# Batch index 1: the weight forms' first additions behind the remainder of g, and one cast moved to ACT

## The chip, the core and the metric

The kernel runs on one core of a Trainium2 chip. The metric is the device time of one execution in microseconds. The engines are TensorE (PE; its weight loads are listed apart as PEld), VectorE (DVE), ScalarE (ACT), GpSimd (POOL, unused but for setup) and SyncE (SP, which issues DMAs).

## The reference: an attention with 32 memories, then a gated product

For 8 batches of 8 heads, 576 rows and width 64, an attention first condenses keys and values with weights from `phi`, and then attends to the 32 condensed memories. Its output, as 4608 rows of 512, goes through two weight matrices with a silu between:

```
a = exp(phi - max(phi));  a = a / (sum(a) + 1e-9)
k_m, v_m = a^T k, a^T v                       # 32 memories per head
scores = q k_m^T / 8
attn = exp(scores - max(scores));  attn = attn / (sum(attn) + 1e-9)
x = attn v_m                                  # 4608 x 512
h = x @ w_in                                  # 512 x 2048
g = h * (1 / (1 + exp(-h)))
out = g @ w_out                               # 2048 x 512
```

The product of attention with `v_m` and `w_in` is folded: the kernel multiplies the memories' values with `w_in` once per batch (a tile `pm`) and the attention's weights with that.

## The kernel before

Every factor of the large products is held as a high part (rounded to PE's fast 32-bit type) and a low part (the remainder), and a product is three: high x high, high x low, low x high. So each tile is first cast and then subtracted: the cast gives the high part, the subtraction the remainder.

A batch runs over 16 steps `fc` of 128 columns of the hidden width. In a step PE computes h (L698, twelve products); ACT takes silu of 512 rows into `gbuf` (L725) and of the 64 left-over rows into `gleft` (L727); `split` makes the two parts of g in `gparts` (L715 the cast on DVE, L717 the remainder on DVE; L713 would be the cast on ACT); one step later PE multiplies g with the matching rows of `w_out`, held as `wo_hi` and `wo_lo` (L743, twelve products: for each of four row tiles high x high, high x low, low x high, so the third product is the first that needs the remainder). h has one buffer: the next step's L698 can start when everything that reads h has read it.

Between these, the next batch's attention is worked off by a table of events, each with a batch and a step (a half is the step's second part). In batch 1 that is, for batch 2: the maximum and the exponent of phi (L258 to L319), the condensed keys and values (L335, L353 to L361, written beside h in h's own buffer), their transposition (L367 on PE, also beside h, then L368 and L369), the scores (L382, L389, L391), their maximum (L426), subtraction (L430), exponent (L434), sum (L438 to L440), division (L444), transposition (L464), and the split of the result (L472 on ACT, L479 on DVE). `p_mm` (L646) and its split (L674 on ACT, L676 on DVE) make `pm`.

Batches 2 to 7 use a form of the second product with fewer multiplications, which needs sums and differences of blocks of `w_out`. They are made in batch 1 by `w_forms`, for eight pairs of row tiles j = 0 to 7. Part 0, at the step 1.5 j + 2, is all on DVE: L811 restores 128 x 1024 weights from their two parts into `wf`, and L815 to L818 make four blocks of 128 x 256 from it. Part 1, at the step 1.5 j + 2.5, splits the result: ACT casts (L832) and DVE subtracts (L833), first one piece `t1` that is then stored in memory, then the pieces `kept`.

What sets the order: PE runs in the written order throughout. ACT does so from batch 1 on (`in_order(ACT)`), so an instruction of `w_forms` that waits on ACT holds up the next silu. In batch 0 DVE and ACT are held in order at its start, and later only by pairs. DVE in batch 1 is ordered by a scheduler when the program is built, within the dependencies; `behind(i, other)` adds a pure order between two instructions of one engine, with no wait. `last_split` is the list of all remainders of g written so far; its last entry is the newest.

Of the kernel before, what the change touches and what calls it, by code (L numbers as in the profile page):

```python
# [25 lines left out]
NFC = DFF // P  # L26
# [22 lines left out]
def attn_ffn_kernel(  # L49
# [37 lines left out]
    def load(dst, src, few=False, queue=None):  # L87
        i = (queue or nc.sync).dma_start(dst, src)
        if few:
            tc.add_manual_dep(  # L90
                i.ins,
                loads[-DEEP].ins.name,
                mybir.DependencyInfo(mybir.DependencyClass.Sync, mybir.DependencyReason.DATA),
                reason="few at a time",
            )
        loads.append(i)

    @contextmanager
    def in_order(*engines):
        traced = nc.cur_bb.bb.instructions  # L100
        n = len(traced)
        last = {}
        yield last
        for i in list(nc.cur_bb.bb.instructions)[n:]:
            if i.engine in engines:
                if i.engine in last:
                    tc.add_manual_dep(
                        i,
                        last[i.engine].name,
                        mybir.DependencyInfo(mybir.DependencyClass.NoSync, mybir.DependencyReason.DATA),  # L110
                        reason="in_order",
                    )
                last[i.engine] = i
# [6 lines left out]
    raws, cvas, last_silu, last_split, last_kvn, last_turn = {}, {}, [], [], [], []  # L120
# [562 lines left out]
    def ffn1(b, fc, h=None, low_last=False):  # L683

        hi, lo = pj[b, fc * P // JW]
        fs = slice(fc * P % JW, fc * P % JW + P)
        ahi, alo = at[b]["ahi"], at[b]["alo"]
        if h is None:
            h = live["h"] = ps.tile([P, 2, 512], F32, tag="h", name="h", bufs=1)
        kinds = ((hi, ahi), (hi, alo), (lo, ahi))  # L690
        todo = [(hf, k) for hf in range(2) for k in range(3)]
        if low_last:
            todo = [(hf, k) for k in (0, 2, 1) for hf in range(2)]
        n = [0, 0]
        for hf, k in todo:
            wt, a = kinds[k]
            for p in range(2):
                nc.tensor.matmul(  # L698
                    h[:, hf, :HALF], wt[:, p, fs], a[:, p, hf * HALF : (hf + 1) * HALF],
                    start=n[hf] == 0, stop=n[hf] == 5, skip_group_check=low_last,  # L700
                )
                n[hf] += 1
        return h
# [3 lines left out]
    def split(g32, steps=(0, 1), gs=None):  # L707
        if gs is None:
            n = next(turn) % 2
            gs = gparts[:, 0, n], gparts[:, 1, n]  # L710
        ghi, glo = gs
        if 2 in steps:
            nc.scalar.activation(ghi, g32, AF.Copy)  # L713
        if 0 in steps:
            nc.vector.tensor_copy(ghi, g32)  # L715
        if 1 in steps:
            last_split.append(nc.vector.tensor_tensor(glo, g32, ghi, op=ALU.subtract))  # L717
        return gs
# [3 lines left out]
    def silu(b, fc, h):  # L722
        g32 = gbuf.rearrange("p (n f) -> p n f", n=2)[:, next(half) % 2]
        w = MAIN // 2
        nc.scalar.activation(g32.rearrange("p (h f) -> p h f", h=2), h[:, :, :w], AF.Silu)  # L725
        o = b % 2 * LEFT
        i = nc.scalar.activation(  # L727
            gleft[:, fc, o : o + LEFT].rearrange("p (h f) -> p h f", h=2), h[:, :, w:HALF], AF.Silu
        )
        if b == 0 and fc > 1:  # L730
            last_silu.append(i)
        return g32
# [61 lines left out]
    def as_f32(x):  # L794
        return x.bitcast(F32)

    def keep(tag, n):
        t = sb.tile([P, n, DMODEL], F32R, tag=tag, name="kept", bufs=1)
        for i in range(n):
            kept.append(t[:, i])  # L800
            kept_at.append((t, i))

    def w_forms(j, step):


        if step == 0:
            while len(kept) < 3 * j + 3:
                keep(*homes_left.pop(0))
            f = at[0]["forms", j] = sb.tile([P, 2, DMODEL], F32, tag="cva", name="wf", bufs=1)
            c = slice(2 * j, 2 * j + 2)  # L810
            i = nc.vector.tensor_tensor(f, as_f32(wo_hi[:, c]), as_f32(wo_lo[:, c]), op=ALU.add)  # L811
            if j == 0:
                behind(i.ins, last_split[-1])
            b11, b12, b21, b22 = (f[:, k, q * Q : (q + 1) * Q] for k in range(2) for q in range(2))
            nc.vector.tensor_tensor(b11, b12, b11, op=ALU.subtract)  # L815
            nc.vector.tensor_tensor(b12, b22, b12, op=ALU.add)
            nc.vector.tensor_tensor(b22, b22, b11, op=ALU.add)
            nc.vector.tensor_tensor(b21, b22, b21, op=ALU.subtract)  # L818
            return
        f = at[0]["forms", j].rearrange("p k (q f) -> p (k q) f", q=2)  # L820
        t1 = sb.tile([P, 1, DMODEL], F32R, tag="cva1", name="t1", bufs=1)
        runs = [[t1, 0, 1]]
        for u in range(3 * j, 3 * j + 3):
            t, i = kept_at[u]
            if t is runs[-1][0]:
                runs[-1][2] = i + 1
            else:
                runs.append([t, i, i + 1])
        n = 0
        for t, i, e in runs:  # L830
            src, to = f[:, n : n + e - i], t[:, i:e]
            nc.scalar.activation(to[:, :, :Q], src, AF.Copy)  # L832
            nc.vector.tensor_tensor(to[:, :, Q:], src, to[:, :, :Q], op=ALU.subtract)  # L833
            n += e - i
        load(saved[j], as_f32(t1[:, 0]))
# [285 lines left out]
    with in_order(DVE, ACT) as last:  # L1121
# [71 lines left out]
        h = ffn1(0, 0, low_last=True)  # L1193
        g32 = silu(0, 0, h)
        w_conv(I1, None, "s")
        gs = split(g32, steps=(2,))
# [24 lines left out]
    def behind(i, other):  # L1221
        tc.add_manual_dep(
            i,
            other.ins.name,
            mybir.DependencyInfo(mybir.DependencyClass.NoSync, mybir.DependencyReason.DATA),
            reason="behind",
        )
# [30 lines left out]
    for b in range(B):  # L1258
        if b == 1:
            whole.close()  # L1260
            ctx.enter_context(in_order(ACT))
        for s in range(NFC if b > 1 else 0):
            t, j = divmod(s, NP)
            h = ffn1s(b, t, j)
            part = forms(b, t, j, h)
            run(b, s)
            finish(range(NI))
            prev = ("st", b, t, j, part)
        for fc in range(NFC if b < 2 else 0):
            if b == 0 and fc < 2:  # L1270
                for part in range(2):
                    for fn, a in events.pop((b, fc + part / 2), []):
                        fn(*a)
                continue
            h = ffn1(b, fc, low_last=b == 1 and fc == 0)
            gs = split(silu(b, fc, h))
            for part in range(2):
                if b == 0:
                    finish((2 * part, 2 * part + 1))
                traced = nc.cur_bb.bb.instructions  # L1280
                n = len(traced)
                late = set()
                for fn, a in events.pop((b, fc + part / 2), []):
                    m = len(nc.cur_bb.bb.instructions)
                    fn(*a)
                    if fn is phi_max:
                        late.update(i.name for i in list(nc.cur_bb.bb.instructions)[m:])
                if b == 0:
                    for i in list(nc.cur_bb.bb.instructions)[n:]:
                        if i.engine == ACT:  # L1290
                            behind(i, last_silu[-1])
                        elif i.engine == DVE and (fc > 10 or i.name in late):
                            behind(i, last_split[-1])
            if b:
                finish(range(NI))
            prev = ("main", b, fc, gs)
        if b % 2:
            for n in range(NLS):
                gs = left_split(b, n)
                if b > 1:  # L1300
                    run(b, NFC + n)
                finish((0, 1, 2, 3))
                prev = ("left", b, n, gs)
# [56 lines left out]
```

## Time and profile before

| | |
|---|---|
| median of three runs | 679.07 us (678.88 to 679.44) |
| the profiled execution | 679.03 us, of it 677.2 us from the first to the last instruction |
| PE busy | 667.9 us |
| DVE busy | 517.8 us |
| ACT busy | 369.1 us |
| mean granted PE clock | 0.999 |

In the profile a row of a list in order of time gives the start in us from the first instruction, the duration, engine, line, operation, the tile written and those read, the shape, and in brackets idle time ahead of it with what ended it. A row with x2 or x12 is that many alike in a row; the duration runs from the first's start to the last's end. Instructions of DVE and ACT can start a little before the one ahead has ended. Batch 1's steps take from about 106 to 189 us, and its left-over rows follow until about 202 us.

### The profile page before, as it was taken

What the parts mean: (1) busy time and instruction counts of PE and PEld (TensorE: products, weight loads), DVE (VectorE), ACT (ScalarE), POOL (GpSimd) and SP (SyncE); (2) the same over time, 40 slices, a digit from 0 to 9 for tenths busy, and PEclk for the clock granted to TensorE, in tenths of its full rate; (3) what the DMA queues carried; (4) which work ended last, traced back from release to release, by engine and by line L of the source; (5) the groups of instructions that cost most, each with busy time, mean ns of one, the idle gap of its engine ahead of it and who ended that gap; (6) DMA issues with size and microseconds to landing.
All of it is one profiled execution on the core that took longest, in us unless ns stands there. A gap on an engine that the chain in (4) does not pass through costs nothing.

```text
span 677.2 us, 14529 instructions
## 1 busy us (share of the span) xinstructions
PE 667.9 (99%) x5788; PEld 588.4 (87%) x5788; DVE 517.8 (76%) x1090; ACT 369.1 (54%) x682; POOL 0.7 (0%) x6
## 2 busy tenths in 40 slices
PE   8999999999999999999999999999999999999997
PEld 3578778787888998999988999899997999889996
DVE  4897899988938689868877688877877668867653
ACT  3878684533625556654655546564654646554441
POOL 0000000000000000000000000000000000000000
PEclk9999999999999999999999999999999999999999
DMA  9988985224270452243520534116430204300001
GB/s 338 373 321 293 313 307 184 82 109 145 85 231 18 185 180 102 79 180 124 178 95 16 184 102 177 66 48 231 157 126 32 86 2 156 114 27 17 32 1 47
DMA packets 37747, 93.92 MB, mean 139 GB/s; under 512 B 4656, under 2 KB 21168, under 8 KB 34096
## 3 DMA queue, kind: packets, MB, share of 16 engines
q1 hardware_dynamic: 36736, 90.22, 38.3%
q10 hardware_dynamic: 944, 2.77, 1.0%
q8 instruction: 46, 0.75, 0.5%
q14 instruction: 21, 0.17, 0.1%
HBM read 77.22 MB, written 15.73 MB: 137 GB/s over the span
## 4 chain that ended last, share of the span: by engine, by line
PE 78%; DVE 6%; ACT 1%; issue 1%; DVEq 0%; ACTq 0%
PE sum L890 34%; PE h L851 21%; PE acc L743 6%; PE lsum L972 5%; PE bg L646 3%; PE h L698 3%; PE accleft L743 2%; PE h L335 1%; PE bg L335 1%; PE bg L382 1%; PE pacc L646 1%; DVE gparts L717 1%; DVE pm L676 0%; DVE sc L430 0%; ACT aparts L879 0%
## 5 line engine op out<-in xcount | busy, mean ns | idle before, releaser
L851 PE MATMUL h<-aparts,pm 128*128 128x288 f32 x1152 | 168.7, 295 | 0.0
L851 PEld LDWEIGHTS h<-aparts,pm 128*128 128x128 f32 x1152 | 157.3, 188 | 0.7
L865 ACT ACTIVATE gbuf<-h 128x512 f32<-128x512 f32 x96 | 57.3, 597 | 117.2 <-PE h L851 113.9
L890 PE MATMUL sum<-wo_hi,aparts 128*128 128x256 f32 x384 | 102.5, 289 | 0.0
L890 PE MATMUL sum<-kept,aparts 128*128 128x256 f32 x576 | 100.1, 282 | 0.0
L890 PE MATMUL sum<-wo_lo,aparts 128*128 128x256 f32 x384 | 100.0, 282 | 0.0
L870 DVE TENSOR_TENSOR gbuf<-gbuf 128x256 f32<-128x256 f32 x96 | 40.6, 423 | 71.4 <-ACT gbuf L865 70.9
L879 ACT ACTIVATE aparts<-gbuf 128x512 fp32r<-128x512 f32 x86 | 54.4, 633 | 63.5 <-DVE gbuf L874 63.5
L743 PE MATMUL acc<-wo_hi,gparts 128*128 128x512 f32 x256 | 85.0, 397 | 0.2
L890 PEld LDWEIGHTS sum<-wo_hi,aparts 128*128 128x128 f32 x384 | 72.7, 189 | 11.5 <-ACT gleft L867 10.1
L890 PEld LDWEIGHTS sum<-kept,aparts 128*128 128x128 f32 x576 | 82.6, 191 | 0.0
L881 DVE TENSOR_TENSOR gparts<-gbuf,aparts 128x512 fp32r<-128x512 f32 x86 | 59.6, 693 | 19.6 <-ACT aparts L879 19.6
L890 PE MATMUL sum<-wo_hi,gparts 128*128 128x256 f32 x384 | 73.2, 281 | 0.0
L890 PEld LDWEIGHTS sum<-wo_lo,aparts 128*128 128x128 f32 x384 | 73.1, 190 | 0.0
L890 PE MATMUL sum<-kept,gparts 128*128 128x256 f32 x288 | 65.5, 282 | 0.0
L743 PEld LDWEIGHTS acc<-wo_hi,gparts 128*128 128x128 f32 x256 | 47.6, 188 | 14.2 <-DVE t L833 1.7
L890 PEld LDWEIGHTS sum<-wo_hi,gparts 128*128 128x128 f32 x384 | 59.4, 190 | 0.0
L698 PEld LDWEIGHTS h<-aparts,pm 128*128 128x128 f32 x372 | 51.8, 188 | 6.5 <-issue 2.7
L698 PE MATMUL h<-aparts,pm 128*128 128x288 f32 x372 | 56.1, 299 | 0.4 <-ACT aparts L611 0.4
L869 ACT ACTIVATE aparts<-gbuf 128x384 fp32r<-128x384 f32 x96 | 50.4, 525 | 0.0
L743 PE MATMUL acc<-wo_lo,gparts 128*128 128x512 f32 x128 | 49.4, 393 | 0.3 <-DVE wo_lo L182 0.2
L890 PEld LDWEIGHTS sum<-kept,gparts 128*128 128x128 f32 x288 | 47.9, 190 | 0.0
(212 smaller groups left out, 954.3 us busy)
## 6 DMA issues: line engine op xcount, KB each, us to landing
win<-win_saved SPq DMA_DIRECT2D x24, 1024.0 KB, 4.9
kv<-in_kv SPq DMA_DIRECT2D x28, 516.0 KB, 4.9
q<-in_q SPq DMA_DIRECT2D x16, 576.0 KB, 6.3
raw<-in_w_in SPq DMA_DIRECT2D x14, 512.0 KB, 7.5
raw<-in_w_out SPq DMA_DIRECT2D x6, 1024.0 KB, 6.6
win_saved<-win SPq DMA_DIRECT2D x4, 1024.0 KB, 8.7
phi<-in_phi SPq DMA_DIRECT2D x7, 576.0 KB, 8.5
out<-oo SPq DMA_DIRECT2D x26, 128.0 KB, 2.3
```

What stands on the lines that cost most here:

```text
L335: nc.tensor.matmul(pt[p][M * r : M * (r + 1), :KVW], e[:, p, c, M * r : M * (r + 1)], kvt[c][:, p, r], start=c == 0, stop=False, skip_grou ...
L646: nc.tensor.matmul((bg[p][M * r : M * (r + 1)] if beside else bg[M * r : M * (r + 1), p, :w]).rearrange("p (k f) -> p k f", f=P), kvT[D * ...
L698: nc.tensor.matmul(h[:, hf, :HALF], wt[:, p, fs], a[:, p, hf * HALF : (hf + 1) * HALF], start=n[hf] == 0, stop=n[hf] == 5, skip_group_chec ...
L743: nc.tensor.matmul(acc[key], gt[:, cs], wt[:, fc], start=fc == 0 and n == 0, stop=fc == NFC - 1 and n == 2)
L851: nc.tensor.matmul(h[:, i, :HALF], wt[:, p, f : f + P], a[:, p], start=n == 0, stop=n == 5)
L865: nc.scalar.activation(gbuf[:, :MAIN].rearrange("p (i f) -> p i f", i=2), h[:, :, :w], AF.Silu)
L869: nc.scalar.activation(hi[:, :3], g[:, 1:4], AF.Copy)
L870: nc.vector.tensor_tensor(g[:, 4:6], g[:, :1].broadcast_to([P, 2, P]), g[:, 1:3], op=ALU.subtract)
L879: nc.scalar.activation(hi[:, 3:], g[:, 4:], AF.Copy)
L881: last_split.append(nc.vector.tensor_tensor(lo[:, 3:], g[:, 4:], hi[:, 3:], op=ALU.subtract))
L890: nc.tensor.matmul(sums[bank][:, place * Q : (place + 1) * Q], gt[:, k], wt, start=bank not in begun, stop=True, skip_group_check=True,)
L972: nc.tensor.matmul(sums[k], part[gt][:, 2 * i + k], wt[:, fc], start=n == 0 and i == 0 and m == 0, stop=last and i == 1 and m == 2,)
```

## The change

Two edits. First, L811 of every j is put behind the newest remainder of g, where before only that of j = 0 was. Second, in the last step of the first batch, the cast of g is made by ACT (L713) and not by DVE; the remainder stays on DVE.

```diff
@@ w_forms, step 0
             i = nc.vector.tensor_tensor(f, as_f32(wo_hi[:, c]), as_f32(wo_lo[:, c]), op=ALU.add)
-            if j == 0:
-                behind(i.ins, last_split[-1])
+            behind(i.ins, last_split[-1])
@@ the loop over the steps of batches 0 and 1
             h = ffn1(b, fc, low_last=b == 1 and fc == 0)
-            gs = split(silu(b, fc, h))
+            gs = split(silu(b, fc, h), steps=(2, 1) if b == 0 and fc == NFC - 1 else (0, 1))
```

PE's and SP's orders stay as they were. After the change every line from L813 on has a number lower by one (L815 to L818 are L814 to L817, L833 is L832).

On ACT, at the end of the first batch, the order before was this (`gbuf` is silu of the 512 rows, `gleft` of the left-over ones, `aparts` the parts of the attention's weights):

```order
L725 ACTIVATE gbuf<-h 128x512
L472 ACTIVATE aparts<-aT_1102 128x2x288
L727 ACTIVATE gleft<-h 128x64
L725 ACTIVATE gbuf<-h 128x512
L757 ACTIVATE o<-acc_397 128x512
```

and it is now:

```order
L725 ACTIVATE gbuf<-h 128x512
L472 ACTIVATE aparts<-aT_1102 128x2x288
L727 ACTIVATE gleft<-h 128x64
L713 ACTIVATE gparts<-gbuf 128x512
L725 ACTIVATE gbuf<-h 128x512
```

The cast stands behind the last silu of batch 0 and ahead of the first of batch 1; on DVE the matching L715 is gone, and L717 follows L479.

On DVE, around the form j = 4 in steps 8 and 9 (`t_1605` is the piece that is stored, `wf` the restored weights and their blocks), the order before was:

```order
L811 TENSOR_TENSOR wf<-wo_hi,wo_lo 128x1024
L815 TENSOR_TENSOR wf<-wf 128x256
L816 TENSOR_TENSOR wf<-wf 128x256
L715 CAST gparts<-gbuf 128x512
L817 TENSOR_TENSOR wf<-wf 128x256
L717 TENSOR_TENSOR gparts<-gbuf,gparts 128x512
L818 TENSOR_TENSOR wf<-wf 128x256
L833 TENSOR_TENSOR t_1605<-wf,t_1605 128x256
L833 TENSOR_TENSOR kept<-wf,kept 128x2x256
L833 TENSOR_TENSOR kept<-wf,kept 128x256
```

and now:

```order
L715 CAST gparts<-gbuf 128x512
L717 TENSOR_TENSOR gparts<-gbuf,gparts 128x512
L811 TENSOR_TENSOR wf<-wo_hi,wo_lo 128x1024
L814 TENSOR_TENSOR wf<-wf 128x256
L815 TENSOR_TENSOR wf<-wf 128x256
L832 TENSOR_TENSOR t_1605<-wf,t_1605 128x256
L816 TENSOR_TENSOR wf<-wf 128x256
L817 TENSOR_TENSOR wf<-wf 128x256
L832 TENSOR_TENSOR kept<-wf,kept 128x2x256
L832 TENSOR_TENSOR kept<-wf,kept 128x256
```

The three additions that stood ahead of the cast of g stand behind both instructions of g, and the stored piece's subtraction stands ahead of the last two additions.

On DVE, around j = 6 in step 11 (`sc` are the scores, `smx` their maximum), before:

```order
L389 STREAM_TRANSPOSE sc_1703<-h 128x64 x2
L391 STREAM_TRANSPOSE sc_1703<-bg 128x512 x2
L811 TENSOR_TENSOR wf<-wo_hi,wo_lo 128x1024
L426 TENSOR_REDUCE smx<-sc_1703 128x36
L815 TENSOR_TENSOR wf<-wf 128x256
L715 CAST gparts<-gbuf 128x512
L816 TENSOR_TENSOR wf<-wf 128x256
L717 TENSOR_TENSOR gparts<-gbuf,gparts 128x512
L817 TENSOR_TENSOR wf<-wf 128x256
L430 TENSOR_TENSOR sc_1703<-sc_1703,smx 128x1152
L818 TENSOR_TENSOR wf<-wf 128x256
```

and now:

```order
L389 STREAM_TRANSPOSE sc_1703<-h 128x64 x2
L391 STREAM_TRANSPOSE sc_1703<-bg 128x512 x2
L426 TENSOR_REDUCE smx<-sc_1703 128x36
L430 TENSOR_TENSOR sc_1703<-sc_1703,smx 128x1152
L715 CAST gparts<-gbuf 128x512
L717 TENSOR_TENSOR gparts<-gbuf,gparts 128x512
L811 TENSOR_TENSOR wf<-wo_hi,wo_lo 128x1024
L814 TENSOR_TENSOR wf<-wf 128x256
L815 TENSOR_TENSOR wf<-wf 128x256
L832 TENSOR_TENSOR t_1776<-wf,t_1776 128x256
L816 TENSOR_TENSOR wf<-wf 128x256
L817 TENSOR_TENSOR wf<-wf 128x256
```

L811 and all additions of the form stand behind the scores' maximum and subtraction and behind g. At j = 1, 2, 3, 5 and 7 L811 passes the cast and the remainder in the same way: where it stood between the two or ahead of both, it now stands behind both.

## The prediction

> **What bounds the kernel now.** I read the page first, then the busy times of one stretch, then the rows in order of time of PE, DVE and ACT in batch index 1, since every edit lies at its start or in it. I write fc(n) for step n of that batch, silu(n), g(n) and h(n) for what belongs to it, and j for the eight weight forms. Line numbers are those of the kernel before.
>
> ```profile
> span 677.2 us, 14529 instructions
> PE 667.9 (99%) x5788; PEld 588.4 (87%) x5788; DVE 517.8 (76%) x1090; ACT 369.1 (54%) x682; POOL 0.7 (0%) x6
> ...
> 104.00:206.00 102.00, 101.84 (x717) 82.65 (x716) 82.30 (x162) 45.56 (x89) 0.00 (x0) 1.00 0.42 142
> ```
>
> PE is the bound. In the 102 us around batch 1 (third row: PE, PEld, DVE, ACT) it is never off, but DVE is busy for 82.3 us of them: there, DVE work that is late reaches PE. The clock is granted in full. PE loses time in this batch at two places only, seen by comparing steps. The rows give each step's first product (L743) and the next h (L698).
>
> ```profile
> 107.86 0.40 PE L743 MATMUL acc<-wo_hi,gparts 128*128 128x512 f32 x1
> 108.56 0.30 PEld L743 LDWEIGHTS acc<-wo_hi,gparts 128*128 128x128 f32 x2 [0.50 <-DVE gparts L717]
> 110.94 1.75 PE L698 MATMUL h<-aparts,pm 128*128 128x288 f32 x12
> ...
> 122.42 0.39 PE L743 MATMUL acc<-wo_hi,gparts 128*128 128x512 f32 x1
> 125.17 1.76 PE L698 MATMUL h<-aparts,pm 128*128 128x288 f32 x12
> 126.77 0.40 PE L743 MATMUL acc<-wo_hi,gparts 128*128 128x512 f32 x1
> 127.50 0.30 PEld L743 LDWEIGHTS acc<-wo_hi,gparts 128*128 128x128 f32 x2 [0.54 <-DVE gparts L717]
> 129.91 1.75 PE L698 MATMUL h<-aparts,pm 128*128 128x288 f32 x12
> ```
>
> An undisturbed step of twelve products takes 125.17 - 122.42 = 2.75 us. The first batch's last takes 110.94 - 107.86 = 3.08 and fc(4)'s 129.91 - 126.77 = 3.14. So the two waits for the remainder of g (L717) cost 0.33 and 0.39 us: 0.72 is the most that the change can win.
>
> **The cast.** DVE loses one cast of 0.42 us, ACT gains one of about 0.63 (the group of the same size and type).
>
> ```profile
> 107.29 0.42 DVE L715 CAST gparts<-gbuf 128x512 fp32r<-128x512 f32 x1
> ...
> 108.12 0.60 ACT L725 ACTIVATE gbuf<-h 128x512 f32<-128x512 f32 x1 [2.02 <-PE h L698]
> 108.86 0.69 DVE L258 TENSOR_TENSOR mt<-phi 128x512 f32<-128x512 f32 x1 [0.35 <-DMA phi<-in_phi]
> ...
> L879 ACT ACTIVATE aparts<-gbuf 128x512 fp32r<-128x512 f32 x86 | 54.4, 633 | 63.5 <-DVE gbuf L874 63.5
> ```
>
> ACT has 2.02 us idle just there, so its 0.63 is covered; without that cover it would delay silu(0) by 0.63. L717 can start about 0.45 earlier, and the stall of 0.33 goes: -0.33, bounds -0.33 and 0. By the Trainium skill (Perfetto Trace Analysis, Optimizing Scalar/DVE Operations) an operation that either engine can do is quicker on DVE where a fast mode exists, and worth moving when DVE is full; the rows have both halves (0.42 against 0.63, and a full DVE), and by that rule -0.33 would be kept to the end.
>
> It is not kept. L258 waits for a DMA, and from there DVE runs without a gap up to the cast of g(2) at 118.92; ACT's next steps hang on that run.
>
> **The additions, j = 1 and 2.** The forms of j = 0 stand behind L717 already, so its rows are the template of what the new order makes of the others: L715, L717, L811, L815 to L818, then ACT's copies (L832), then the next silu.
>
> ```profile
> 118.29 0.60 ACT L725 ACTIVATE gbuf<-h 128x512 f32<-128x512 f32 x1 [3.45 <-PE h L698]
> 118.92 0.43 DVE L715 CAST gparts<-gbuf 128x512 fp32r<-128x512 f32 x1
> 119.45 0.69 DVE L717 TENSOR_TENSOR gparts<-gbuf,gparts 128x512 fp32r<-128x512 f32 x1
> 120.06 1.22 DVE L811 TENSOR_TENSOR wf<-wo_hi,wo_lo 128x1024 f32<-128x1024 f32 x1
> 123.53 0.85 ACT L832 ACTIVATE kept<-wf 128x768 fp32r<-128x768 f32 x1 [1.34 <-DVE wf L818]
> 124.28 0.58 ACT L725 ACTIVATE gbuf<-h 128x512 f32<-128x512 f32 x1
> ```
>
> From one silu to the next that is 124.28 - 118.29 = **5.99 us**, set by DVE and ACT, while a PE step takes 2.75 + 1.60 (the twelve h products, 126.77 - 125.17) = 4.35. A form in this order makes the next silu 1.64 us late unless PE has other work in the step.
>
> At j = 1, L717 passes L811, which frees L717 by L811's spacing, 1.22 less an overlap of 0.08: the stall of 0.39 goes. Of the 0.72 now won, ACT lets through only a part:
>
> ```profile
> 129.26 0.22 ACT L727 ACTIVATE gleft<-h 128x64 f32<-128x64 f32 x1
> 131.75 0.60 ACT L725 ACTIVATE gbuf<-h 128x512 f32<-128x512 f32 x1 [1.14 <-PE h L698]
> 131.82 1.22 DVE L811 TENSOR_TENSOR wf<-wo_hi,wo_lo 128x1024 f32<-128x1024 f32 x1
> 137.34 0.35 DVE L361 TENSOR_SCALAR kvn<-h,rs 128x128 f32<-128x128 f32 x1 [0.43 <-ACT kvn L359]
> 137.75 1.86 PE L698 MATMUL h<-aparts,pm 128*128 128x288 f32 x12
> ```
>
> h(5) at 129.91 needs L727 done (129.48), which hangs on the same DVE run and gains 0.1 to 0.2; so PE is 0.4 to 0.5 early. Then j = 2: L811 used to start at 131.82, while DVE waited for silu(5). Now DVE starts with L715 when silu(5) ends, 131.75 - 0.5 + 0.63 = 131.9, and the same instructions follow up to L361, with 0.3 us more of gaps, since L717 now stands right behind its cast and L815 right behind L811 (dependent neighbours start 0.04 to 0.1 after the end, independent ones 0.08 before it). L361 comes at 137.3 to 137.7, and h(6), which needs it, at 137.7 to 138.1. **The 0.72 is gone: -0.1 to +0.3 here; I take 0.** j = 3 has cover: its additions start behind g(6), and its copies on ACT stand only behind silu(7), a step later.
>
> **j = 4.**
>
> ```profile
> 147.01 1.22 DVE L811 TENSOR_TENSOR wf<-wo_hi,wo_lo 128x1024 f32<-128x1024 f32 x1
> 148.35 0.60 ACT L725 ACTIVATE gbuf<-h 128x512 f32<-128x512 f32 x1 [2.57 <-issue]
> 150.80 0.94 ACT L832 ACTIVATE kept<-wf 128x512 fp32r<-128x512 f32 x2 [1.43 <-DVE wf L818]
> 152.63 0.60 ACT L725 ACTIVATE gbuf<-h 128x512 f32<-128x512 f32 x1 [0.90 <-PE h L698]
> 153.55 0.44 PE L367 MATMUL h<-ident,kvn 128*128 128x128 f32 x2
> ...
> PEld h L367 <- ACT gleft L727: 0.8, 1, 0.8
> ```
>
> L811 ran before silu(8); now it waits for L717 of g(8). By the template, with the copy in two pieces (0.94 for 0.85), silu(9) starts at 148.35 + 6.08 = 154.43 instead of 152.63. L727 ends 0.72 after a silu's start (0.60 + 0.22 less an overlap of 0.1): 155.15. PE's transposition of kvn (L367) waits for just that L727 (the row from the list of waits), and behind it on PE stands the whole of fc(8)'s product. With 0.1 to start, L367 comes at 155.25, not 153.55: **+1.7** (1.25 to 2.0 with the bounds above).
>
> **j = 5 to 7 and the end.** DVE just keeps pace at j = 5. From L389 on it has no reserve:
>
> ```profile
> 161.37 0.37 DVE L389 STREAM_TRANSPOSE sc<-h 128x64 f32<-128x64 f32 x2
> 168.44 0.42 DVE L818 TENSOR_TENSOR wf<-wf 128x256 f32<-128x256 f32 x1
> 170.50 0.42 DVE L715 CAST gparts<-gbuf 128x512 fp32r<-128x512 f32 x1
> 170.83 1.22 DVE L811 TENSOR_TENSOR wf<-wo_hi,wo_lo 128x1024 f32<-128x1024 f32 x1
> ...
> 183.10 1.36 DVE L479 TENSOR_TENSOR aparts<-aT,aparts 128x1152 fp32r<-128x1152 f32 x1 [0.66 <-ACT aparts L472]
> 186.18 0.68 DVE L717 TENSOR_TENSOR gparts<-gbuf,gparts 128x512 fp32r<-128x512 f32 x1
> ...
> 186.92 0.73 PE L743 MATMUL acc<-wo_hi,gparts 128*128 128x512 f32 x2
> ```
>
> L389 to L818's end took 168.86 - 161.37 = 7.49, gapless. The new order has L426 and L430 (the scores' maximum and its subtraction) and both g instructions ahead of L811, puts the third piece's subtraction (L833, 0.34 of spacing) ahead of L817, and makes six or seven neighbours dependent, 0.9 in all: 8.7. So L818 ends at 161.37 + 1.7 + 8.7 = 171.8, +2.9, and ACT's copies, silu(12) and the cast of g(12) behind it are +2.9. At j = 7 L811 changes places with L717: its start was 0.33 behind L715, and is now 0.53 + 0.60 = 1.13 behind it: +3.7. From there to the end of L717 of g(15) the same instructions follow (186.86 - 170.83 = 16.0, of it 0.66 idle, for a copy that itself waits for DVE): +0.1 for gaps. L717 ended at 186.86 and PE's third product came at 186.92 and lost 0.1: no cover. **PE is 3.8 us late after batch 1.** Behind it no edit lies, and a PE that is busy for 99% carries a shift to the end.
>
> The sum on the profiled execution: 677.2 + 3.8 = 681.0 of span, 679.03 + 3.8 = 682.8 in time; the median, 679.07, gives 682.9. I take 682.8. With the bounds at h(6) and L367 it is 3.3 to 4.5: 682.3 to 683.5.
>
> **Rivals.** (A) *DVE packs better than I let it.* From silu(8) on DVE gets 2.06 us of additions that ran ahead of it (L811 and two of the short ones, 1.22 + 2 x 0.42) and about 1.1 of gaps at four forms (0.3 at each of three, and the third piece); it had 1.72 us idle here:
>
> ```profile
> 159.07 0.43 DVE L715 CAST gparts<-gbuf 128x512 fp32r<-128x512 f32 x1 [1.72 <-ACT gbuf L725]
> ```
>
> If it can use all of that, 2.06 + 1.1 - 1.72 = +1.4: 680.5; with a part of it, 680.5 to 682. For it: much here is two engines taking turns, and 0.1 in a hand-over counts ten times. Against it: the orders are fixed, and ACT's copies bar the next silu whatever DVE could do.
>
> (B) *The change does what its two places promise, not slower.* Both stalls go and the additions' later start is covered everywhere: 679.07 - 0.72 = 678.4. It is decided at silu(9): if it starts by 152.7 (153.55 less L727's 0.72 and 0.1), L367 is on time. For it: DVE is idle for 20 of 102 us. Against: 5.99 against a step of 4.35, measured in this very order. By the Trainium skill (Perfetto Trace Analysis, Optimization Strategy) one finds what ends the gaps of the contended engine and makes that come sooner; by that rule the time is this 678.4. The trace agrees on both gaps, and shows at 137.75 and 153.55 what comes late in their place.
>
> (C) *Each hand-over costs more than I took.* From silu(8) to the end the new path changes engine about ten times; with 0.1 more at each, +1.0: 683.8. For it speaks that nothing on this path has slack left; against it, that the template's 5.99 has its hand-overs in it.
>
> That the change does nothing can't be: the built order shows L811 moved at seven forms.
>
> **Numbers.** Forecast 0.66, A 0.18, B 0.10, C 0.06. This kernel tells no change from one within 0.2% (1.36 us): 677.7 to 680.4. Forecast, C and nearly all of A lie above: slower 0.86; B and the foot of A are within it: same 0.12; faster 0.02, since only 0.72 is there to win. Range 680.6 to 683.9.
>
> **What would show it.** In the changed profile: no wait for L717 at 108 and 127; h(6) near 137.75; silu(9) 1.7 us late, with its wait put down to DVE's last addition, and L367 waiting for L727; silu(12) 2.9 us late; a wait for L717 of g(15), and everything behind it some 3.8 us later. If silu(9) is on time, the forecast is wrong from there on; if only the end is on time, A holds.

## The result and the profile after

The changed kernel takes 682.91 us (median of six runs, 682.85 to 683.18), against 679.12 for the kernel before (six runs, 678.85 to 679.44): a ratio of 1.0056, with a 95% interval of 1.0046 to 1.0067. It is 3.8 us slower.

The page of the changed kernel, and its busy times (PE, PEld, DVE, ACT, POOL) in the same 102 us:

```profile
span 681.1 us, 14525 instructions
PE 667.8 (98%) x5788; PEld 588.0 (86%) x5788; DVE 519.0 (76%) x1089; ACT 369.1 (54%) x683; POOL 0.7 (0%) x6
...
104.00:206.00 102.00, 98.65 (x679) 79.70 (x678) 81.88 (x158) 43.28 (x84) 0.00 (x0) 1.00 0.39 136
```

PE does the same work (667.8 us busy for 667.9) in a span that is 3.9 us longer, and in this window it is busy for 98.65 us and not 101.84. The granted clock is 1.00 in this window in both.

Lines from L813 on have numbers lower by one here. PEld rows show how long a weight load waits; the products can lose less than that (before, the waits of 0.50 and 0.54 us cost 0.33 and 0.39). First the two places that were to be won, and what came after each, in order of time:

```profile
108.47 0.41 PEld L743 LDWEIGHTS acc<-wo_hi,gparts 128*128 128x128 f32 x2
...
125.14 1.62 PEld L698 LDWEIGHTS h<-aparts,pm 128*128 128x128 f32 x12 [0.21 <-ACT gleft L727]
127.07 0.42 PEld L743 LDWEIGHTS acc<-wo_hi,gparts 128*128 128x128 f32 x2
129.64 1.49 PEld L698 LDWEIGHTS h<-aparts,pm 128*128 128x128 f32 x11 [0.32 <-ACT gleft L727]
...
137.62 0.35 DVE L361 TENSOR_SCALAR kvn<-h,rs 128x128 f32<-128x128 f32 x1
138.03 1.19 PE L698 MATMUL h<-aparts,pm 128*128 128x288 f32 x7 [0.27 <-DVE kvn L361]
```

Neither load of the third product waits any more (0.50 and 0.54 us before). But now h(4) and h(5) wait for ACT's L727, and h(6) for DVE's L361. Then j = 4:

```profile
148.63 0.60 ACT L725 ACTIVATE gbuf<-h 128x512 f32<-128x512 f32 x1 [2.58 <-PE h L698]
150.41 1.22 DVE L811 TENSOR_TENSOR wf<-wo_hi,wo_lo 128x1024 f32<-128x1024 f32 x1
153.88 0.94 ACT L831 ACTIVATE kept<-wf 128x512 fp32r<-128x512 f32 x2 [1.29 <-DVE wf L817]
154.72 0.58 ACT L725 ACTIVATE gbuf<-h 128x512 f32<-128x512 f32 x1
155.46 0.44 PE L367 MATMUL h<-ident,kvn 128*128 128x128 f32 x2 [1.57 <-ACT gleft L727]
```

From silu(8) to silu(9) it takes 154.72 - 148.63 = 6.09 us (the template with the copy in two pieces said 6.08). ACT's copy L831 stands 1.29 us for DVE's last addition (L817), silu(9) follows the copy at once, and PE stands for 1.57 us until L727 of that step is done. And the end of the batch:

```profile
163.27 0.37 DVE L389 STREAM_TRANSPOSE sc<-h 128x64 f32<-128x64 f32 x2
171.67 0.43 DVE L817 TENSOR_TENSOR wf<-wf 128x256 f32<-128x256 f32 x1
172.98 0.58 ACT L725 ACTIVATE gbuf<-h 128x512 f32<-128x512 f32 x1
174.88 1.22 DVE L811 TENSOR_TENSOR wf<-wo_hi,wo_lo 128x1024 f32<-128x1024 f32 x1
...
179.14 1.63 PEld L698 LDWEIGHTS h<-aparts,pm 128*128 128x128 f32 x12 [0.93 <-ACT gleft L727]
190.10 0.50 PE L743 MATMUL acc<-wo_hi,gparts 128*128 128x512 f32 x1 [0.79 <-DVE gparts L715]
190.30 0.68 DVE L717 TENSOR_TENSOR gparts<-gbuf,gparts 128x512 fp32r<-128x512 f32 x1
191.04 0.30 PEld L743 LDWEIGHTS acc<-wo_hi,gparts 128*128 128x128 f32 x2 [0.64 <-DVE gparts L717]
```

From L389 to the end of the form's last addition DVE takes 172.10 - 163.27 = 8.83 us (7.49 before). Then h(14) waits for ACT, and the last step of the batch waits first for the cast (L715) and then for the remainder (L717) of g(15).

**Where PE lost it.** Both kernels have the same 5788 products in the same order, so the start of each product can be set against that of the same one before. Two executions differ by up to half a microsecond from their first loads on (the products before the 108 us mark are shifted by +0.37 here, and by -0.5 to +0.5 in the kernels below), so the table takes each kernel's shift at 107.9 us off. Positive is later than in the kernel before, and a negative number is PE's lead over it, in us. The columns are places in the time of the kernel before: behind the first stall (109.5) and the second (128.5), behind h(5) (131.3) and h(6) (139), ahead of L367 (152) and behind it (156), ahead of h(13) and h(14) (170) and behind them (177.5), behind the last step's first wait (186.3) and its second (188), in batch 2 (243.5), and near the end (660).

| kernel | 109.5 | 128.5 | 131.3 | 139 | 152 | 156 | 170 | 177.5 | 186.3 | 188 | 243.5 | 660 |
|---|---|---|---|---|---|---|---|---|---|---|---|---|
| the change | -0.35 | -0.68 | -0.51 | -0.09 | -0.10 | 1.53 | 1.53 | 2.31 | 3.26 | 3.77 | 3.50 | 3.47 |

The two gains are there in full (-0.68), are gone at h(6) (-0.09), and the loss comes in three places: 1.63 at L367, 0.78 at h(14), 1.46 in the last step. Some 0.27 come back at 243 us, in batch 2.

### The profile page after: what moved, and what is told of

It is laid out like the page before. It is cut to its first block, busy times and chain, and to the rows that moved or that the text cites. A ratio compares the mean times of both kernels' runs of the same rounds, so it can differ in the third digit from the quotient of the medians.

```text
span 681.1 us, 14525 instructions
## 1 busy us (share of the span) xinstructions
PE 667.8 (98%) x5788; PEld 588.0 (86%) x5788; DVE 519.0 (76%) x1089; ACT 369.1 (54%) x683; POOL 0.7 (0%) x6
## 4 chain that ended last, share of the span: by engine, by line
PE 83%; DVE 7%; ACT 2%; issue 2%; DVEq 0%; ACTq 0%
PE sum L889 34%; PE h L850 22%; PE acc L743 8%; PE h L698 5%; PE lsum L971 5%; PE bg L646 3%; PE accleft L743 2%; PE bg L335 1%; PE bg L382 1%; DVE gparts L717 1%; PE h L335 1%; DVE pm L676 1%; DVE wf L811 1%; PE pacc L646 1%; DVE kept L832 0%
```

## The experiments

Every kernel starts from the kernel before and keeps its line numbers, unless it says that it starts from the change. The same table for all of them comes at the end of this section.

### The cast alone

```diff
-            gs = split(silu(b, fc, h))
+            gs = split(silu(b, fc, h), steps=(2, 1) if b == 0 and fc == NFC - 1 else (0, 1))
```

> The second edit alone; only j = 0 stays behind the remainder of g. Theory (the prediction's): the stall at 108 us goes (0.33 us), but DVE's gapless run from the DMA of phi on, and ACT behind it, take 0.2 or more of it back; 678.8 to 679.1. Rival 'both gains are kept': 678.8 or less, with PE 0.33 us early at 190 us. Rival 'the cast does the harm': 682 to 683.

679.02 us (eleven runs, 678.59 to 679.49) against 679.04; the ratio is 1.0 (0.9991 to 1.0009). The weight loads of PE show where the 0.33 went: all but 0.06 at h(4), a step earlier than the prediction's text has it. The last step of the batch, a place that I had not expected, then takes 0.24 more, so that PE is 0.19 late behind it.

```profile
125.03 1.09 PEld L698 LDWEIGHTS h<-aparts,pm 128*128 128x128 f32 x8 [0.39 <-ACT gleft L727]
...
187.15 0.30 PEld L743 LDWEIGHTS acc<-wo_hi,gparts 128*128 128x128 f32 x2 [0.48 <-DVE gparts L717]
```

The kernel before already has a wait of 0.26 us at that last load. The further 0.2 have their origin on DVE. Its run up to L717 of g(15) starts with the cast of g(10), which waits for silu(10), and in this kernel that run keeps the times of the kernel before (-0.04 aligned) up to L816 of j = 6. L717 of g(11), the next on DVE, starts 0.54 us after L816 here (165.92 to 166.46) and 0.33 us after it in the kernel before (165.90 to 166.23), in the same order. Every instruction of DVE from there to L717 of g(15) is late by the same 0.2 us. The profiled executions of the kernels "j = 0, 1", "copies of 0 later" and "and g(14)" below show the same delay; those of the kernel before, "j = 0 to 5", "and g(5)" and "copies alone" do not. What causes it is open, and with one trace of each kernel it isn't known whether every execution has it.

### The order alone

```diff
-            if j == 0:
+            if j >= 0:
                 behind(i.ins, last_split[-1])
```

> The first edit alone, for all eight forms; the cast stays on DVE. Theory: the whole loss, 682.8 to 683.2, a little above the change's 682.9, since the 0.1 to 0.2 us that the cast gives DVE are missing. Rival 'the cast does the harm': 679.

682.77 us (five runs, 682.43 to 683.21) against 679.04: 1.0053 (1.0040 to 1.0066). The whole loss is in the first edit. I had expected a median a little above the change's; it is a hair below. In the aligned traces this kernel is 0.38 later (3.85 against 3.47). The spread of the runs does not tell such a difference.

### Behind the remainder for j = 0 and 1 only

```diff
-            if j == 0:
+            if j < 2:
                 behind(i.ins, last_split[-1])
```

with the cast on ACT as in the change.

> Both edits, but the additions stand behind the remainder of g for j = 0 and 1 only. Theory: both stalls (0.72 us) are gone and nothing is late later, but PE's lead is cut to 0.4 or 0.5 us at h(5) by ACT and to 0.1 or 0.2 at h(6) by DVE (L361): 678.9 to 679.0, L367 at its place, no wait at the end. Rival 'the promised gain is there once the other forms stay': 678.4.

679.10 us (eleven runs, 678.83 to 679.64): a ratio of 1.0 (0.9991 to 1.0009). L367 is at its place. PE's lead goes as expected from -0.65 to -0.48 at h(5) and -0.21 at h(6). "No wait at the end" was wrong: the last step takes the remaining 0.23, as with the cast alone, and as there DVE's run had come 0.2 later at L717 of g(11). So the two wins of the change, without its harm, are worth nothing in these runs. What takes them back is ACT's L727 at h(4) and h(5), DVE's L361 at h(6), and in this trace DVE's L717 of g(15).

### All forms but j = 4

```diff
-            if j == 0:
+            if j != 4:
                 behind(i.ins, last_split[-1])
```

with the cast on ACT as in the change.

> The whole change, but for j = 4, whose additions stand where they stood before. Theory: silu(9) and L367 are on time, 1.7 us come back, and the 2.1 us from j = 6 and 7 at the end of the batch stay: 681.0 to 681.4. Rival 'each moved form costs its share' (3.8 us over six forms, 0.6 each): 682.2. Rival 'j = 4 is all of it': 679.1.

680.98 us (seven runs, 680.72 to 681.80) against 679.07: 1.0029 (1.0018 to 1.0040). L367 is on time, and the end is late by itself. PE's weight loads in the last step:

```profile
187.94 0.19 PEld L743 LDWEIGHTS acc<-wo_hi,gparts 128*128 128x128 f32 x1 [1.22 <-DVE gparts L715]
188.88 0.30 PEld L743 LDWEIGHTS acc<-wo_hi,gparts 128*128 128x128 f32 x2 [0.64 <-DVE gparts L717]
```

So j = 4 is worth 682.91 - 680.98 = 1.9, neither the 0.6 nor the whole loss of the two rivals.

### Forms 0 to 5 only

```diff
-            if j == 0:
+            if j < 6:
                 behind(i.ins, last_split[-1])
```

with the cast on ACT.

> Both edits, with the additions behind the remainder of g for j = 0 to 5. Theory: L367 is 1.7 us late as in the change, and j = 6 and 7 add nothing, because DVE keeps its old order from there on: 680.6 to 681.0. Rival 'each moved form costs its share': 682.9 - 1.2 = 681.7. Rival 'the lateness at j = 4 is made up by DVE's and ACT's idle time later': 679.5 or less.

680.51 us (ten runs, 680.06 to 681.07): 1.0020 (1.0010 to 1.0030), 0.1 below the expected range. The list of waits of PE's loads from 104 to 210 us has L367's wait for L727, and for L717 of g(15) no more than the kernel before has (0.26):

```profile
PEld h L367 <- ACT gleft L727: 2.5, 1, 2.5
...
PEld acc L743 <- DVE gparts L717: 0.3, 1, 0.3
```

What L367 loses (1.64 in the aligned traces) is neither made up later nor does it grow.

### Forms 0, 1 and 6 only

```diff
-            if j == 0:
+            if j in (0, 1, 6):
                 behind(i.ins, last_split[-1])
```

with the cast on ACT.

> Both edits, with the additions behind the remainder of g for j = 0, 1 and 6 only. Theory: L367 on time; DVE without reserve from L389 on, so L818 of j = 6 and silu(12) are 1.2 us late or more and L717 of g(15) is late by 1.2 to 2: 680.3 to 681.0. Rival 'each moved form costs its share' (0.6): 679.5.

680.41 us (ten runs, 680.10 to 681.60): 1.0020 (1.0011 to 1.0030). One form, j = 6, moves the time by 1.3 over the kernel with j = 0 and 1: its additions stand in the stretch from L389 on, in which DVE has no reserve. With the two kernels above, "each form costs its share" has fallen.

### The change, with ACT's copies of j = 4 half a step later

This one starts from the change.

```diff
-                ev(b, 1.5 * j + 2.5, w_forms, j, 1)
+                ev(b, 1.5 * j + (3 if j == 4 else 2.5), w_forms, j, 1)
```

> The whole change, but ACT's copies of the form j = 4 and their subtractions come half a step later, behind silu(9) and not ahead of it. Theory: ACT no longer bars silu(9), L367 comes at 153.6 and not 155.3, and PE has no stall there; but DVE still gets that form's 2 us of additions late, so the end of the batch is late by 3 to 3.5 us all the same: 682.2 to 682.6. Rival 'ACT's wait alone is the price': 682.9 - 1.7 = 681.2, and the end late by only 2 us.

682.33 us (four runs, 682.11 to 682.44): 1.0047 (1.0032 to 1.0062). Here ACT's rows and PE's:

```profile
152.72 0.60 ACT L725 ACTIVATE gbuf<-h 128x512 f32<-128x512 f32 x1 [3.61 <-issue]
154.68 0.41 ACT L831 ACTIVATE t<-wf 128x256 fp32r<-128x256 f32 x1
...
153.58 0.44 PE L367 MATMUL h<-ident,kvn 128*128 128x128 f32 x2
...
189.46 0.19 PEld L743 LDWEIGHTS acc<-wo_hi,gparts 128*128 128x128 f32 x1 [1.50 <-DVE gparts L715]
190.39 0.30 PEld L743 LDWEIGHTS acc<-wo_hi,gparts 128*128 128x128 f32 x2 [0.64 <-DVE gparts L717]
```

silu(9) no longer waits for the copies, L367 starts at 153.58 without a wait, and yet 0.6 us of 3.8 are won. The stall that L367 had comes back: PE waits 0.33 us at h(13), 0.83 at h(14), and 1.08 and 0.20 in the last step. So ACT's bar at j = 4 is what stops PE first, but without it DVE's late work still makes nearly all of the loss: PE has to wait for g(15) whether it was stopped before or not. The subtractions of j = 4 on DVE move with the copies here, so this run doesn't tell the late additions from the late subtractions.

### Versions that are better than both

From the kernel with j = 0 and 1, the copies of j = 0 were moved half a step later, behind silu(3); then g(14), and g(5) as well, were cast by ACT. The lines below show what the last of them adds, set against the kernel before; the order for j < 2 and the first batch's cast on ACT are in all three.

```diff
-                ev(b, 1.5 * j + 2.5, w_forms, j, 1)
+                ev(b, 1.5 * j + (2.5 if j else 3), w_forms, j, 1)
...
-            gs = split(silu(b, fc, h), steps=(2, 1) if b == 0 and fc == NFC - 1 else (0, 1))
+            gs = split(silu(b, fc, h), steps=(2, 1) if (b, fc) in ((0, NFC - 1), (1, 5), (1, NFC - 2)) else (0, 1))
```

The first step alone:

> As the version with j = 0 and 1 only, and ACT's copies of the form j = 0 and their subtractions come half a step later, behind silu(3) and not ahead of it. Theory: ACT's wait for DVE's last addition no longer holds silu(3) up, so the limit at h(5) goes and PE keeps more of its lead: 678.4 to 678.7. Rival 'DVE alone sets the pace up to h(6)': no better than the version with j = 0 and 1, 678.9 to 679.0.

678.43 us (eleven runs, 678.28 to 678.99) against 679.04: 0.9989 (0.9980 to 0.9998). ACT's limit at h(4) and h(5) is gone; h(6) and the last step still take their part, 0.22 and 0.24.

```profile
129.39 1.74 PEld L698 LDWEIGHTS h<-aparts,pm 128*128 128x128 f32 x12
...
137.67 1.49 PEld L698 LDWEIGHTS h<-aparts,pm 128*128 128x128 f32 x11 [0.48 <-DVE kvn L361]
...
187.07 0.30 PEld L743 LDWEIGHTS acc<-wo_hi,gparts 128*128 128x128 f32 x2 [0.49 <-DVE gparts L717]
```

With the cast of g(14) on ACT:

> The version whose copies of j = 0 come later, and in addition ACT casts g(14) of batch 1. In that version PE came to the last step of batch 1 0.54 us early and gave back 0.24 there, waiting for L717 of g(15) at the end of a DVE run. Theory (DVE's run is the last gate): without the cast of 0.42 (0.34 of spacing) the run ends 0.3 earlier and the 0.24 is kept: 678.1 to 678.3. Rival 'the gate is ACT's copy of the attention's weights (L472) and not DVE': no change, 678.4.

678.26 us (eleven runs, 677.87 to 678.75) against 678.98: 0.9989 (0.9980 to 0.9998). The medians alone don't tell it from the version before it; the aligned traces do: the last step takes nothing any more (-0.52 at 186.3, -0.62 at 188), and no load waits for L717 there. So by the traces the rival, ACT's copy L472, is not the gate.

With that of g(5) too:

> As the version with g(14) cast by ACT, and g(5) cast by ACT too, which takes 0.34 us off DVE's run to L361. Theory: PE gave back 0.2 us at h(6) for L361, and keeps it now, if the end of the batch lets it through: 677.9 to 678.2. Rival 'the end of the batch is the only gate': as without it, 678.1 to 678.3.

677.78 us (eleven runs, 677.29 to 678.25) against 678.98: 0.9983 (0.9974 to 0.9992), a little better than expected. Both waits shown for the first step, at h(6) and in the last step, are gone:

```profile
136.63 1.70 PEld L698 LDWEIGHTS h<-aparts,pm 128*128 128x128 f32 x12
...
187.01 0.41 PEld L743 LDWEIGHTS acc<-wo_hi,gparts 128*128 128x128 f32 x2
```

And the later copies of j = 0 in the kernel before, with nothing else:

> The kernel before, with one move alone: ACT's copies of the form j = 0 and their subtractions half a step later. Neither edit of the change is in it. Theory: the wait at 127 us goes without the order at j = 1 too, since silu(3) and with it g(3) come about 1.7 us earlier; the stall of 0.33 at 108 stays: 678.5 to 678.8. Rival 'the change's two edits are needed for it': 679.0 to 679.1.

678.57 us (eleven runs, 678.18 to 679.02) against 678.98: 0.9996 (0.9987 to 1.0005). The interval does not tell it from no change. The aligned traces show the gain of the stall at 127 us (-0.36 at 128.5) without any order behind L717 at j = 1, and h(6) taking half of it. PE's lead of 0.17 ahead of the last step is 0.12 behind it. That the move is worth something in time is not shown by these runs alone.

### The shifts of all kernels

| kernel | median, us | 109.5 | 128.5 | 131.3 | 139 | 152 | 156 | 170 | 177.5 | 186.3 | 188 | 243.5 | 660 |
|---|---|---|---|---|---|---|---|---|---|---|---|---|---|
| cast alone | 679.02 | -0.32 | -0.06 | -0.05 | -0.04 | -0.04 | -0.04 | -0.05 | -0.05 | -0.05 | 0.19 | 0.18 | 0.27 |
| order alone | 682.77 | 0.01 | -0.36 | -0.23 | 0.20 | 0.19 | 1.81 | 1.80 | 2.59 | 3.56 | 4.08 | 3.84 | 3.85 |
| j = 0, 1 | 679.10 | -0.34 | -0.65 | -0.48 | -0.21 | -0.21 | -0.21 | -0.23 | -0.23 | -0.23 | 0.02 | 0.01 | -0.03 |
| all but 4 | 680.98 | -0.33 | -0.72 | -0.54 | -0.11 | -0.11 | -0.11 | -0.11 | 0.67 | 1.63 | 2.16 | 1.91 | 1.87 |
| j = 0 to 5 | 680.51 | -0.35 | -0.47 | -0.32 | 0.11 | 0.11 | 1.75 | 1.75 | 1.75 | 1.75 | 1.80 | 1.82 | 1.80 |
| j = 0, 1, 6 | 680.41 | -0.34 | -0.73 | -0.59 | -0.33 | -0.33 | -0.33 | -0.33 | 0.45 | 1.13 | 1.63 | 1.37 | 1.31 |
| change, copies of 4 later | 682.33 | -0.34 | -0.47 | -0.32 | 0.11 | 0.11 | 0.11 | 0.13 | 1.82 | 3.07 | 3.57 | 3.30 | 3.45 |
| copies of 0 later | 678.43 | -0.35 | -0.73 | -0.75 | -0.53 | -0.53 | -0.53 | -0.54 | -0.54 | -0.54 | -0.30 | -0.56 | -0.57 |
| and g(14) | 678.26 | -0.32 | -0.71 | -0.72 | -0.49 | -0.51 | -0.51 | -0.52 | -0.52 | -0.52 | -0.62 | -0.88 | -0.88 |
| and g(5) | 677.78 | -0.34 | -0.73 | -0.74 | -0.85 | -0.86 | -0.86 | -0.86 | -0.86 | -0.86 | -0.97 | -1.24 | -1.24 |
| copies alone | 678.57 | 0.02 | -0.36 | -0.37 | -0.16 | -0.17 | -0.17 | -0.17 | -0.17 | -0.17 | -0.12 | -0.37 | -0.25 |

## Why the prediction was right

It forecast 682.8 and slower; 682.9 was measured. The steps of its sum are borne out one by one below. That the two figures agree to 0.1 us is in part luck: in the aligned traces PE ends 3.47 late and not 3.8, and the start's shift of 0.37, which lies ahead of the first place that the edits touch, makes up the rest of the profiled span.

- **What there was to win** was sized at 0.72: 0.68 by 128.5 us in the change, 0.35 of it by the cast. Right. That PE loses time "at two places only" was not exact: in the last of the better versions PE gains about 0.1 more at h(6) (-0.74 to -0.85) and in the last step (-0.86 to -0.97).
- **The cast's 0.33 "is not kept"**, since DVE's run from the phi DMA and ACT behind it set the pace: the cast alone shows that it isn't kept, and that ACT's L727 takes it. The place was a step too late in the text (h(5); it is h(4) that waits, 0.39 us, when the cast is alone).
- **PE 0.4 to 0.5 early at h(5), and 0 at h(6)** (-0.1 to +0.3): 0.51 early and -0.09. Right.
- **j = 4**, the template's 6.08 from silu to silu and 1.7 at L367: 6.09 and 1.63. Right, and its cause is shown: without j = 4 L367 is on time, and with only ACT's copies of j = 4 moved it is too.
- **j = 6 and 7**, DVE without reserve: 8.7 us forecast from L389 to the last addition, 8.83 measured; silu(12) late by 2.9, measured 172.98 - 169.74 less the start's 0.37, 2.9; L811 of j = 7 late by 3.7, measured 174.88 - 170.83 less the start's 0.37, 3.7. Right. In the prediction PE waits for this only in the last step; in the run 0.78 of it is met earlier, at h(14). The sum is the same, since the last step waits for the same DVE run.
- **3.8 late after batch 1**: 3.77. "PE carries a shift to the end" was right but for 0.27 us that come back at 243 us.
- **The rivals.** A (DVE packs better, 680.5 to 682) did not come about: DVE took 8.83 us for the run that the forecast put at 8.7, no less. B (678.4) rested on cover that isn't there; the kernel with j = 0 and 1 shows that even its two gains alone end at 679.1. By the Trainium skill (Perfetto Trace Analysis, Optimization Strategy) the dependency that ends a gap is made to come sooner; the trace agrees that the gaps closed, and shows that other limits stood close behind: with j = 0 and 1 PE's lead of 0.65 is 0.48 behind h(5) and 0.21 behind h(6). C (hand-overs dearer by 0.1) isn't seen: 6.09 against 6.08.

What it did not see is what a lead of PE meets in the last step. It counted 0.1 us of waiting for L717 of g(15) there as a loss of the kernel before, and not as a limit on a lead. The limit is not a fixed one: DVE's run up to it starts behind silu(10) and moves with PE, and with the copies alone only 0.05 of the lead is taken. In the kernels in which the last step takes 0.24, DVE's run had come 0.2 later at L717 of g(11). For the change this made no difference; for the better versions it did.

## What to carry to other kernels

A stall of PE at one instruction tells what is late there, not what is next. Look for the next engine's slack before counting the gain, step by step until the end of the stage. Work without a due time that fills idle time on a busy engine (here DVE's additions ahead of a cast) is not harmless to postpone. It can then fall into a stretch without reserve, and an engine whose order is fixed (here ACT) and that waits for it passes the delay on to work that has nothing to do with it. Where the new order already stands somewhere in the program, as at j = 0 here, its rows give the price of the change almost exactly.

## What the runs showed that I had not expected

Taking away the stall at L367 gave back 0.6 us of 3.8, although PE lost 1.63 there: two causes, ACT's bar at j = 4 and DVE's late work, cover each other. DVE's late work without that bar still makes 3.3 of the 3.8; no run has the bar with DVE's work of j = 4 on time. By the Trainium skill (Perfetto Trace Analysis, Optimizing Scalar/DVE Operations) moving work from a full DVE to ScalarE may pay. The trace agrees for some places only: the same 0.42 us cast is worth 0.0 us in time at the first batch's end, and the two at g(5) and g(14) together 0.65 us (678.43 to 677.78), where DVE was the gate. At g(14) the gate was there in part by the 0.2 us that DVE had lost at g(11). The 0.27 us that come back in batch 2, at 243 us, are a wait: in the kernel before, the cast alone, j = 0 and 1, and j = 0 to 5, ACT stands 0.16 or 0.17 us ahead of L924 with no releaser in the profile, and PE's L382 then 0.19 or 0.20 us for the silu behind it (L867). In the other nine kernels both are absent. Why they are is open; it wasn't tried.
